# Bucket codes beside the second burst of sums over V, and softmax denominators by chunk

## The chip, the cores and the metric

The kernel runs as one program on one core of a Trainium2 chip. The metric is the device time of one execution in microseconds (us), median of three runs. TensorE is called PE here (PEld for its weight loads), VectorE DVE, ScalarE ACT, GpSimd POOL; SP issues most DMAs. A time in a trace is counted from the start of the profiled span.

## The reference, cut to what matters

Attention in which a query sees only the keys of its own hash bucket, then two gated two-matrix layers on the result. B, H, S, D are 2, 8, 768, 64.

```python
q_bits = (np.einsum('bhsd,dk->bhsk', q, proj) > 0)      # 6 bits each; the same for k
mask = q_bucket[:, :, :, None] == k_bucket[:, :, None, :]
scores = np.where(mask, scale * q @ k.T, -1e9)
attn = np.exp(scores - scores.max(-1))
attn = attn / (attn.sum(-1) + 1e-9)
x = (attn @ v)                                          # to (1536, 512)
h = x @ w_in; x = (h * np.tanh(softplus(h))) @ w_out    # first layer, d_ff 2048
h = x @ w2_in; x = (P(h) / (Q(h) + 1e-6)) @ w2_out      # second layer, P cubic, Q quadratic
```

The result has 1536 rows of 512. Both layers are computed with each operand split into a high and a low part, three products in place of one.

## The kernel before

**Attention.** There are 16 heads, and the work of each is cut into six chunks of 128 keys. `run` goes through slots of time: slot g holds, for every entry of the table `order`, the call whose place falls on g. An entry has the place of head 0, and six slots later comes the next head. So slot 6h + c does chunk c of the scores of head h, and beside it the maxima of a head further on, the sums of the same head some slots late, and the preparation of heads two and three further on. Within a slot the calls are issued in the order of the table, and every engine runs its own instructions in the order in which they were issued. I call the slots of a head 0 to 5; slot 7 of a head is slot 1 of the next.

What a slot issues, by the names that stand in the profile:

- `st` (L373): the tile `sp`, scores with the keys on the partitions, four matmuls of 384 columns (high and low part of the queries, two halves of 384 positions); then ACT takes the exponential into the tile `e`.
- `smax` (L340): the tile `mp`, the same scores with the queries on the partitions, two matmuls; then DVE takes the maximum into `m`.
- `pv` (L391): sums over V of one chunk, out of `e`, two matmuls of 384 columns in float32, each of which writes 64 partitions, so that the two run beside each other in two strips of the array. Three bursts of two chunks each stand in slots 3, 5 and 7 of a head.
- `dsum` (L400): the denominators, the tile `dn`. Four matmuls with a weight of 32 columns of ones stand in four strips of the array. They take two chunks at once, each chunk in two halves of 384 positions; the two halves of partitions are added later by DVE.
- `codes` (L298): the projections of a head's keys and queries, the tile `cp`, in two strips as in `pv`. DVE makes the key rows of it (`code_k`, L320, the tile `kk`), ACT the signs of the query rows (`code_q`, L329, the tile `qB`).
- `vsum` (L268): the sum of V, the tile `vsp`, for two heads together, in slot 3 of every even head; DVE scales it into `vsc`.
- `evac`, `devac`, `gather`, `recip`, `store`, `spread`, `norm`: the results of `pv` and `dn` go out of PSUM, the denominators through two small DMAs (L440) onto 24 partitions, DVE inverts them, and they come back over DRAM.

A float32 matmul stands twice in the trace (two passes), a float32r matmul once. The tiles `sp`, `mp` and `vsp` share a pool of three PSUM buffers: a new tile can be written when the reader of the tile that had its buffer is done, which is ACT for `sp` and DVE for `mp` and `vsp`. The framework decides at build time which buffer a new tile gets; mostly it is the one of three tiles before. `dn` and `cp` share one buffer (L301, L404).

**The layers.** `moe` follows (L632). For each of 3 blocks of 512 rows and 16 slices of d_ff it does 12 matmuls of the first matrix and 12 of the second; the gating runs on ACT and DVE. Beside the first steps DVE rebuilds weights from the 64-bit input (L100 to L106), and `tail` (L626) issues the last slots of attention between them.

The lines that set the places which the change touches:

```python
("lo", lo, -15, 1),
("codes", codes, -16, 1),
("pv", pv, (3, 3, 5, 5, 7, 7), 6),
("dsum", dsum, (5, 5, 5, 5, 7, 7), 6),
("vsum", vsum, 3, 0),
("code_k", code_k, -16, 1),
("code_q", code_q, -14, 1),
```

Of the kernel before, what the change touches and what calls it, by code (L numbers as in the profile page):

```python
# [9 lines left out]
F32 = mybir.dt.float32  # L10
# [3 lines left out]
ACT = mybir.ActivationFunctionType  # L14
ALU = mybir.AluOpType
# [3 lines left out]
B, H, S, D = 2, 8, 768, 64  # L19
# [3 lines left out]
HALF = S // 2  # L23
BLK = 512
NBLK = NT // BLK
NC = S // 128
# [6 lines left out]
    lo="dd", hi="aa", xhi="a", xlo="dd", whi="pppp", wlo="pppp",  # L33
)
C_AT = 16
ROW, TINY = 31, 2.0 ** -60
# [8 lines left out]
def attention_moe_moe(ctx: ExitStack, tc: tile.TileContext, kq, v, proj2, cst, eye, w1, w2, ab, out):  # L45
    nc = tc.nc

    def pool(stack, name, bufs=1, **kw):
        return stack.enter_context(tc.tile_pool(name=name, bufs=bufs, **kw))
# [120 lines left out]
    def attention(actx, tctx):  # L170
        ev_p = pool(tctx, "ev", 2, side="right")
        rx_p = pool(tctx, "rx", 1, side="right")
        cs_p = pool(tctx, "cs", 2, side="right")
# [20 lines left out]
        ones = v_p.tile([128, 32], F32, tag="ones", name="ones")  # L194
# [86 lines left out]
        def qhalf(t, a):  # L281
            return t[:, a * HALF:(a + 1) * HALF]
# [88 lines left out]
        pt = {}  # L371
# [16 lines left out]
        pvt = {}  # L388
# [9 lines left out]


        def dsum(h, c):  # L400
            if not 0 <= h < B * H or c % 2 == 0:
                return
            if c == 1:
                pvt[h, "d"] = pvp.tile([128, 512], F32, tag="dn", name="dn")  # L404
            for n in range(4):
                nc.tensor.matmul(  # L406
                    out=pvt[h, "d"][32 * n:32 * n + 32, 0:HALF], lhsT=ones, rhs=qhalf(pt[h, c - 1 + n // 2], n % 2),
                    start=(c == 1), stop=(c == NC - 1),
                )

        Rt = {}
# [15 lines left out]
        def devac(h):  # L427
            if not 0 <= h < B * H:
                return
            dv = cs_p.tile([128, HALF], F32, tag="dv", name="dv")  # L430
            nc.scalar.activation(out=dv, in_=pvt.pop((h, "d"))[:, 0:HALF], func=ACT.Copy)
            Rt[h] = dv

        def gather(h):
            if not 0 <= h < B * H:
                return
            dv = Rt.pop(h)
            cs = cs_p.tile([24, 2, 32], F32, tag="cs", name="cs")
            for n in range(2):
                nc.sync.dma_start(  # L440
                    out=cs[:, n], in_=dv[64 * n:64 * n + 64:32].rearrange("t (a i) -> t a i", i=32)
                )
            Rt[h] = cs

        def recip(h):
            if not 0 <= h < B * H:
                return
            cs = Rt.pop(h)
            rc = cs_p.tile([24, 32], F32, tag="rc", name="rc")

            z = cs_p.tile([24, 32], F32, tag="z", name="z")
            nc.vector.tensor_tensor(out=rc, in0=cs[:, 0], in1=cs[:, 1], op=ALU.add)
            nc.vector.tensor_scalar(
                out=z, in0=rc, scalar1=0.0, scalar2=float(np.float32(1e-9)) / (S * TINY) - 1.0, op0=ALU.is_equal, op1=ALU.mult
            )
            nc.vector.tensor_scalar(out=rc, in0=rc, scalar1=1e-9, scalar2=None, op0=ALU.add)
            nc.vector.reciprocal(out=rc, in_=rc)
            nc.vector.scalar_tensor_tensor(out=rc, in0=z, scalar=1.0, in1=rc, op0=ALU.add, op1=ALU.mult)
            Rt[h, "r"] = rc
# [52 lines left out]
        for n, p in enumerate(parts):  # L512
            i = W_AT + 6 * n
# [10 lines left out]
        def first(f, n):  # L524
# [18 lines left out]
            ("fin_b", fin_b, -5, 1),  # L543
            ("hi", hi, -18, 1),
            ("move_k", move_k, -17, 1),
            ("lo", lo, -15, 1),
            ("codes", codes, -16, 1),
            ("pv", pv, (3, 3, 5, 5, 7, 7), 6),
            ("dsum", dsum, (5, 5, 5, 5, 7, 7), 6),
            ("vsum", vsum, 3, 0),  # L550
            ("code_k", code_k, -16, 1),
            ("code_q", code_q, -14, 1),
            ("evac", evac, 7, 1),
            ("devac", devac, 7, 1),
            ("gather", gather, 8, 1),
            ("recip", recip, 10, 1),
            ("store", store, 11, 1),
            ("spread", spread, 12, 1),
# [298 lines left out]
    with tc.manual_schedule():  # L857
        nc.scalar.preload_act_table_set("natural_log_exp_and_others")
        tctx = ExitStack()
        with ExitStack() as actx:  # L860
            run, tail = attention(actx, tctx)
            run()
        with ExitStack() as mctx:
            run = moe(mctx, tctx, tail)
            run()
# [55 lines left out]
```

## Time and profile before

| | |
|---|---|
| median of 3 runs | 793.1 us (792.79 to 796.85) |
| profiled execution: time, span | 791.69 us, 789.8 us |
| mean granted TensorE clock | 0.999 |
| busy PE, PEld, DVE, ACT, POOL | 774.2, 572.4, 593.7, 422.5, 71.6 us |

PE has its first matmul of the layers at 259.65 us; what is before that is attention. A busy time counts overlapping instructions once, and matmuls overlap, so the 98% of PE does not say how fast it works. What a group of matmuls costs is read from the start of its first to the start of the next group in the timeline. A row of the timeline is start, time, engine, line, operation, tiles, shapes, count, and in brackets the idle time ahead of it with what ended it; what stands there as a count is of passes.

### The profile page before, as it was taken

The page shows a single profiled execution, that of the slowest core. Times are in us where ns is not written, and L with a number is a line of the kernel's source. Part 1 is how long each engine was busy: PE and PEld are TensorE (multiplying, and loading weights), DVE is VectorE, ACT ScalarE, POOL GpSimd, SP SyncE. Part 2 cuts the span into 40 slices and gives each one's busy share as a digit, 9 for nine tenths or more (in the row PEclk, how much of TensorE's full clock was granted, in tenths as well). Part 3 has the DMA queues.
Part 4 walks back from the last instruction along what each step waited for, and adds up shares of the span by engine and source line. Part 5 has one row for each costly group of instructions (what it writes and reads, how often), then busy time and mean ns, then how long its engine had stood idle before and what let it go on. Part 6 is the DMA issues. An engine that isn't in the chain of part 4 may idle for free.

```text
span 789.8 us, 10934 instructions
## 1 busy us (share of the span) xinstructions
PE 774.2 (98%) x3788; PEld 572.4 (72%) x3788; DVE 593.7 (75%) x1100; ACT 422.5 (53%) x684; POOL 71.6 (9%) x100
## 2 busy tenths in 40 slices
PE   7899999999999999999999999999999999999998
PEld 4556555555555778888888888887888888888886
DVE  5587778778772599846556677659998888888886
ACT  3455565655555443331212334368886867777664
POOL 4223214124121000000000000000000000000000
PEclk9999999999999999999999999999999999999999
DMA  4847666554651444424555587620000100000001
GB/s 124 211 128 202 174 162 175 141 142 121 174 166 31 127 137 148 131 87 145 171 157 149 165 255 256 202 80 1 0 1 1 53 1 1 1 36 18 1 0 54
DMA packets 57031, 85.50 MB, mean 108 GB/s; under 512 B 20496, under 2 KB 28688, under 8 KB 56976
## 3 DMA queue, kind: packets, MB, share of 16 engines
q1 hardware_dynamic: 55952, 84.77, 36.4%
q8 instruction: 30, 0.49, 0.3%
q14 instruction: 25, 0.20, 0.1%
q0 software_dynamic: 1024, 0.03, 0.1%
HBM read 57.71 MB, written 14.73 MB: 92 GB/s over the span
## 4 chain that ended last, share of the span: by engine, by line
PE 88%; DVE 6%; DMA 2%; ACT 1%; issue 1%; SPq 1%; POOL 0%; DVEq 0%; ACTq 0%
PE h L665 29%; PE y L685 16%; PE y L683 15%; PE sp L380 9%; PE pv L287 8%; PE mp L347 5%; PE dn L406 4%; PE cp L287 2%; DVE w L70 1%; DVE m L351 1%; DMA kk<-qB 1%; DVE t L103 1%; DMA vf<-v 1%; DVE r L106 1%; DVE gl L70 1%
## 5 line engine op out<-in xcount | busy, mean ns | idle before, releaser
L665 PE MATMUL h<-xh,w 128*128 128x512 f32 x768 | 205.0, 389 | 0.0
L665 PEld LDWEIGHTS h<-xh,w 128*128 128x128 f32 x768 | 144.1, 188 | 30.6 <-issue 0.6
L351 DVE TENSOR_REDUCE m<-mp 128x1 f32<-128x768 f32 x96 | 91.3, 955 | 50.2 <-PE mp L347 49.0
L385 ACT ACTIVATE e<-sp 128x768 f32<-128x768 f32 x96 | 77.1, 810 | 80.8 <-PE sp L380 79.4
L70 DVE TENSOR_TENSOR gl<-ep,gh 128x512 fp32r<-128x512 f32 x96 | 65.9, 687 | 69.4 <-ACT ep L709 68.6
L708 ACT ACTIVATE gh<-h 128x512 fp32r<-128x512 f32 x48 | 28.7, 598 | 154.7 <-PE h L665 141.5
L665 PE MATMUL h<-xl,w 128*128 128x512 f32 x384 | 102.7, 389 | 0.0
L685 PE MATMUL y<-w,gh 128*128 128x512 f32 x384 | 96.3, 389 | 0.0
L683 PE MATMUL y<-gh,w 128*128 128x512 f32 x384 | 94.8, 389 | 0.0
L665 PEld LDWEIGHTS h<-xl,w 128*128 128x128 f32 x384 | 72.1, 188 | 15.1
L683 PEld LDWEIGHTS y<-gh,w 128*128 128x128 f32 x384 | 72.1, 188 | 15.0
L685 PEld LDWEIGHTS y<-w,gh 128*128 128x128 f32 x384 | 72.1, 188 | 15.0
L287 PE MATMUL pv<-e,vf 128*64 128x384 f32 x384 | 72.5, 499 | 0.0
L380 PE MATMUL sp<-qB,kk 128*128 128x384 f32 x192 | 55.5, 370 | 1.6 <-DMA qB<-stt 1.1
L715 ACT ACTIVATE ep<-h 128x512 f32<-128x512 f32 x48 | 28.5, 595 | 52.3 <-PE h L665 52.3
L347 PE MATMUL mp<-kk,qB 128*128 128x384 f32 x192 | 52.8, 358 | 3.2 <-DVE m L351 2.3
L106 DVE SCALAR_TENSOR_TENSOR r<-r,t 128x256 int32<-128x256 int32 (+1 forms) x114 | 52.2, 457 | 4.7
L380 PEld LDWEIGHTS sp<-qB,kk 128*128 128x128 f32 x192 | 30.8, 188 | 34.1 <-issue 16.0
L103 DVE SCALAR_TENSOR_TENSOR t<-r,t 128x256 int32<-128x256 int32 (+1 forms) x114 | 52.2, 458 | 3.9
L685 PE MATMUL y<-w,gl 128*128 128x512 f32 x192 | 53.3, 392 | 0.5 <-DVE gl L70 0.4
L717 DVE TENSOR_TENSOR n<-n,ep 128x512 f32<-128x512 f32 x48 | 33.1, 690 | 26.9 <-ACT n L716 26.9
L683 PE MATMUL y<-gl,w 128*128 128x512 f32 x192 | 51.6, 390 | 1.6 <-DVE gl L70 1.6
(79 smaller groups left out, 1012.2 us busy)
## 6 DMA issues: line engine op xcount, KB each, us to landing
r<-w SPq DMA_DIRECT2D x100, 256.0 KB
w<-r SPq DMA_DIRECT2D x64, 128.0 KB
w<-w SPq DMA_DIRECT2D x16, 512.0 KB
r<-w SPq DMA_DIRECT2D x14, 512.0 KB
kq<-kq SPq DMA_DIRECT2D x16, 384.0 KB
kk<-qB SPq DMA_DIRECT2D x15, 384.0 KB
kk<-qX SPq DMA_DIRECT2D x16, 192.0 KB
qX<-qB SPq DMA_DIRECT2D x16, 192.0 KB
```

Of the source, the lines that this page charges most:

```text
L70: nc.vector.tensor_tensor(out=o, in0=i, in1=f32(h), op=ALU.subtract)
L103: lambda: nc.vector.scalar_tensor_tensor(out=t, in0=r[:, :, 1], scalar=-0x40000000, in1=t, op0=ALU.bitwise_and, op1=ALU.bitwise_or),
L106: lambda: nc.vector.scalar_tensor_tensor(out=o, in0=r[:, :, 0], scalar=29, in1=t, op0=ALU.logical_shift_right, op1=ALU.bitwise_or),
L287: nc.tensor.matmul(out=o[64 * a:64 * a + 64, 0:HALF], lhsT=w, rhs=qhalf(x, a), start=start, stop=stop)
L347: nc.tensor.matmul(out=p[:, a, 0:HALF], lhsT=qB[h % 4][:, c * 128:(c + 1) * 128], rhs=qhalf(KK[h % 4][:, 0], a), start=True, stop=True,)
L351: nc.vector.tensor_reduce(out=mt[h][:, c:c + 1], in_=halves(p), op=ALU.max, axis=AX.XY)
L380: nc.tensor.matmul(out=p[:, a, 0:HALF], lhsT=kk[:, c * 128:(c + 1) * 128], rhs=qq[:, a * HALF:(a + 1) * HALF], start=(i == 0), stop=(i == 1),)
L385: nc.scalar.activation(out=wide(e), in_=halves(p), func=ACT.Exp, scale=1.0 / D ** 0.5)
L665: nc.tensor.matmul(out=p, lhsT=w[:, c * 128:(c + 1) * 128], rhs=x[:, c, :], start=(n == 0), stop=(n == 11))
L683: nc.tensor.matmul(out=y[m], lhsT=w[:, DM + m * 128:DM + (m + 1) * 128], rhs=g, **s)
L685: nc.tensor.matmul(out=y[m], lhsT=g[:, m * 128:(m + 1) * 128], rhs=w[:, DM:2 * DM], **s)
L717: nc.vector.tensor_tensor(out=v_, in0=v_, in1=u, op=ALU.mult)
```

## The change

`codes` moves from slot 2 to slot 3 of a head, where it is issued directly ahead of the burst of `pv`, and `code_k` and `code_q` move to the same slot. `lo` goes one slot ahead. `dsum` takes one chunk per call, in four quarters of 192 positions, so a head has 24 matmuls of 192 columns in place of 12 of 384. `dv` has 192 columns, `gather` is one DMA in place of two, and the addition of two halves in `recip` is gone.

```diff
-            if not 0 <= h < B * H or c % 2 == 0:
+            if not 0 <= h < B * H:
                 return
-            if c == 1:
+            if c == 0:
                 pvt[h, "d"] = pvp.tile([128, 512], F32, tag="dn", name="dn")
             for n in range(4):
                 nc.tensor.matmul(
-                    out=pvt[h, "d"][32 * n:32 * n + 32, 0:HALF], lhsT=ones, rhs=qhalf(pt[h, c - 1 + n // 2], n % 2),
-                    start=(c == 1), stop=(c == NC - 1),
+                    out=pvt[h, "d"][32 * n:32 * n + 32, 0:S // 4], lhsT=ones,
+                    rhs=pt[h, c][:, n * S // 4:(n + 1) * S // 4], start=(c == 0), stop=(c == NC - 1),
                 )
...
-            cs = cs_p.tile([24, 2, 32], F32, tag="cs", name="cs")
-            for n in range(2):
-                nc.sync.dma_start(
-                    out=cs[:, n], in_=dv[64 * n:64 * n + 64:32].rearrange("t (a i) -> t a i", i=32)
-                )
+            cs = cs_p.tile([24, 32], F32, tag="cs", name="cs")
+            nc.sync.dma_start(out=cs, in_=dv[0:128:32].rearrange("t (a i) -> t a i", i=32))
...
-            nc.vector.tensor_tensor(out=rc, in0=cs[:, 0], in1=cs[:, 1], op=ALU.add)
...
-            ("lo", lo, -15, 1),
-            ("codes", codes, -16, 1),
+            ("lo", lo, -16, 1),
+            ("codes", codes, -15, 1),
             ("pv", pv, (3, 3, 5, 5, 7, 7), 6),
             ("dsum", dsum, (5, 5, 5, 5, 7, 7), 6),
             ("vsum", vsum, 3, 0),
-            ("code_k", code_k, -16, 1),
-            ("code_q", code_q, -14, 1),
+            ("code_k", code_k, -15, 1),
+            ("code_q", code_q, -15, 1),
```

On PE, slots 2 and 3 of a head before. What stands in brackets is what the first matmul of a tile waits for: Activation or DVE is the reader of the tile that had its buffer.

```order
L347 MATMUL mp<-kk_130,qB_122 128x384 [waits Activation_49]
L347 MATMUL mp<-kk_130,qB_122 128x384
L287 MATMUL cp<-kq,pr 64x384 [waits Activation_49]
L287 MATMUL cp<-kq,pr 64x384
L380 MATMUL sp<-qB_120,kk_128 128x384 [waits DVE_49]
L380 MATMUL sp<-qB_120,kk_128 128x384
L380 MATMUL sp<-qX_124,kk_128 128x384 x2
L347 MATMUL mp<-kk_130,qB_122 128x384 [waits Activation_49]
L347 MATMUL mp<-kk_130,qB_122 128x384
L287 MATMUL pv<-e,vf_131 64x384 x4
```

The same place now:

```order
L347 MATMUL mp<-kk_130,qB_122 128x384 [waits Activation_49]
L347 MATMUL mp<-kk_130,qB_122 128x384
L380 MATMUL sp<-qB_120,kk_128 128x384 [waits DVE_49]
L380 MATMUL sp<-qB_120,kk_128 128x384
L380 MATMUL sp<-qX_124,kk_128 128x384 x2
L347 MATMUL mp<-kk_130,qB_122 128x384 [waits Activation_49]
L347 MATMUL mp<-kk_130,qB_122 128x384
L287 MATMUL cp<-kq,pr 64x384 x2
L287 MATMUL pv<-e,vf_131 64x384 x4
```

The two matmuls of `cp` went behind the `mp` of slot 3, so that slots 2 and 3 follow each other as `sp`, `mp`, `sp`, `mp`, and `cp` and `pv` have the same strips.

On PE, slot 5 of the same head before:

```order
L380 MATMUL sp<-qB_120,kk_128 128x384 [waits DVE_49]
L380 MATMUL sp<-qB_120,kk_128 128x384
L380 MATMUL sp<-qX_124,kk_128 128x384 x2
L347 MATMUL mp<-kk_130,qB_122 128x384 [waits Activation_49]
L347 MATMUL mp<-kk_130,qB_122 128x384
L287 MATMUL pv<-e,vf_131 64x384 x4
L406 MATMUL dn<-e,ones 32x384 [waits Activation_49]
```

And now:

```order
L380 MATMUL sp<-qB_120,kk_128 128x384 [waits DVE_49]
L380 MATMUL sp<-qB_120,kk_128 128x384
L380 MATMUL sp<-qX_124,kk_128 128x384 x2
L347 MATMUL mp<-kk_130,qB_122 128x384 [waits DVE_49]
L347 MATMUL mp<-kk_130,qB_122 128x384
L287 MATMUL pv<-e,vf_131 64x384 x4
L406 MATMUL dn<-e,ones 32x192 [waits Activation_49]
```

The `mp` of slot 5 no longer takes the buffer of slot 4's `sp` (three tiles before, read by ACT) but that of slot 4's `mp` (two tiles before, read by DVE). The built program has this in slot 5 of heads 1 to 12. In slot 1 of heads 4, 6, 8, 10 and 12 it is the other way: there `mp` took the buffer of slot 0's `mp` before, and now takes that of slot 0's `sp`.

On DVE, slots 2 to 4 of an even head before; `qX` is `lo`, `kk` is `code_k`:

```order
L351 TENSOR_REDUCE m<-mp 128x1
L324 TENSOR_SCALAR kk_128<-cp,cst 32x384 x2
L351 TENSOR_REDUCE m<-mp 128x1
L70 TENSOR_TENSOR qX_124<-kq,qB_120 128x768
L279 TENSOR_SCALAR vsc<-vsp 128x2
L351 TENSOR_REDUCE m<-mp 128x1
```

And now:

```order
L351 TENSOR_REDUCE m<-mp 128x1
L70 TENSOR_TENSOR qX_124<-kq,qB_120 128x768
L351 TENSOR_REDUCE m<-mp 128x1
L279 TENSOR_SCALAR vsc<-vsp 128x2
L324 TENSOR_SCALAR kk_128<-cp,cst 32x384 x2
L351 TENSOR_REDUCE m<-mp 128x1
```

The two operations of `code_k` and `lo` changed places, and in an even head `code_k` stands behind `vsc`, directly ahead of the maximum of slot 4.

## Rows read from the trace of the kernel before

**Rows 1.** The page, part 4: the chain by engine.

```profile
PE 88%; DVE 6%; DMA 2%; ACT 1%; issue 1%; SPq 1%; POOL 0%; DVEq 0%; ACTq 0%
```

**Rows 2.** Timeline, PE, slots 2 to 5 of an odd head.

```profile
194.24 0.61 PE L380 MATMUL sp<-qB,kk 128*128 128x384 f32 x2
...
195.49 0.87 PE L287 MATMUL cp<-kq,pr 128*64 128x384 f32 x4
196.29 0.62 PE L380 MATMUL sp<-qB,kk 128*128 128x384 f32 x2
...
197.56 1.51 PE L287 MATMUL pv<-e,vf 128*64 128x384 f32 x8
199.00 0.62 PE L380 MATMUL sp<-qB,kk 128*128 128x384 f32 x2
...
200.50 0.51 PE L380 MATMUL sp<-qX,kk 128*128 128x384 f32 x2
200.93 0.62 PE L347 MATMUL mp<-kk,qB 128*128 128x384 f32 x2
201.48 1.51 PE L287 MATMUL pv<-e,vf 128*64 128x384 f32 x8
```

**Rows 3.** Timeline, ACT, two exponentials: slot 4, and slot 0 of an even head.

```profile
200.06 0.81 ACT L385 ACTIVATE e<-sp 128x768 f32<-128x768 f32 x1 [1.88 <-PE sp L380]
...
205.35 0.81 ACT L385 ACTIVATE e<-sp 128x768 f32<-128x768 f32 x1 [0.25 <-PE sp L380]
```

**Rows 4.** Timeline, PE, at three places, in order of time.

```profile
49.10 0.62 PE L347 MATMUL mp<-kk,qB 128*128 128x384 f32 x2
...
186.18 0.61 PE L347 MATMUL mp<-kk,qB 128*128 128x384 f32 x2
...
205.87 0.51 PE L380 MATMUL sp<-qX,kk 128*128 128x384 f32 x2
206.72 0.62 PE L347 MATMUL mp<-kk,qB 128*128 128x384 f32 x2 [0.35 <-DVE m L351]
```

**Rows 5.** Waits in 40 to 240 us: total, times, longest.

```profile
PE mp L347 <- DVE m L351: 1.7, 5, 0.3
```

**Rows 6.** Timeline, ACT, the signs of head 3.

```profile
33.93 1.16 ACT L333 ACTIVATE qB<-cp,cst 32x384 fp32r<-32x384 f32 x2 [3.37 <-DMA kk<-qB]
```

**Rows 7.** Timeline, DVE, at seven places, in order of time.

```profile
43.08 1.82 DVE L351 TENSOR_REDUCE m<-mp 128x1 f32<-128x768 f32 x2 [0.37 <-PE mp L347]
...
184.44 0.16 DVE L279 TENSOR_SCALAR vsc<-vsp 128x2 f32<-128x2 f32 x1
...
196.48 1.34 DVE L324 TENSOR_SCALAR kk<-cp,cst 32x384 fp32r<-32x384 f32 x2
...
198.73 0.95 DVE L70 TENSOR_TENSOR qX<-kq,qB 128x768 fp32r<-128x768 f32 x1
200.35 0.96 DVE L351 TENSOR_REDUCE m<-mp 128x1 f32<-128x768 f32 x1 [0.68 <-PE mp L347]
201.23 0.17 DVE L452 TENSOR_TENSOR rc<-cs 24x32 f32<-24x32 f32 x1
...
205.71 0.96 DVE L351 TENSOR_REDUCE m<-mp 128x1 f32<-128x768 f32 x1 [1.58 <-PE mp L347]
```

**Rows 8.** Timeline, PE: matmuls of 128 columns with a weight of 32 columns.

```profile
14.93 1.50 PE L318 MATMUL wm<-wones,ones 128*32 128x128 f32 x12
```

**Rows 9.** Windows, L406 alone: stretch, length, PE busy and count, PEld the same.

```profile
202.91:202.95 0.04, 0.03 (x4) 0.03 (x5) 1.00 0.95 359
```

**Rows 10.** Timeline, DMA issues of SP, ahead of the first loads of the layers.

```profile
260.68 1.07 SPq L440 DMA_DIRECT2D cs<-dv  x2
261.80 0.88 SPq L774 DMA_DIRECT2D r<-w  x2
```

**Rows 11.** Timeline, DVE, the first rebuilt weights of the layers.

```profile
265.04 0.30 DVE L100 TENSOR_SCALAR t<-r 128x256 int32<-128x256 int32 x1 [0.47 <-DMA r<-w]
```

**Rows 12.** Timeline, PE, a wait in the layers.

```profile
290.79 0.50 PE L683 MATMUL y<-gl,w 128*128 128x512 f32 x1 [1.60 <-DVE gl L70]
```

More of the change, by code (lines that the diff above doesn't have):

```diff
@@ L429, in devac @@
                 return
-            dv = cs_p.tile([128, HALF], F32, tag="dv", name="dv")
-            nc.scalar.activation(out=dv, in_=pvt.pop((h, "d"))[:, 0:HALF], func=ACT.Copy)
+            dv = cs_p.tile([128, S // 4], F32, tag="dv", name="dv")
+            nc.scalar.activation(out=dv, in_=pvt.pop((h, "d"))[:, 0:S // 4], func=ACT.Copy)
             Rt[h] = dv
@@ L451, in recip @@
             z = cs_p.tile([24, 32], F32, tag="z", name="z")
-            nc.vector.tensor_tensor(out=rc, in0=cs[:, 0], in1=cs[:, 1], op=ALU.add)
             nc.vector.tensor_scalar(
-                out=z, in0=rc, scalar1=0.0, scalar2=float(np.float32(1e-9)) / (S * TINY) - 1.0, op0=ALU.is_equal, op1=ALU.mult
+                out=z, in0=cs, scalar1=0.0, scalar2=float(np.float32(1e-9)) / (S * TINY) - 1.0, op0=ALU.is_equal, op1=ALU.mult
             )
-            nc.vector.tensor_scalar(out=rc, in0=rc, scalar1=1e-9, scalar2=None, op0=ALU.add)
+            nc.vector.tensor_scalar(out=rc, in0=cs, scalar1=1e-9, scalar2=None, op0=ALU.add)
             nc.vector.reciprocal(out=rc, in_=rc)
```

## The prediction

> **What bounds the kernel now.** I read the page's chain first: 88% of the time that ends last is PE's, 6% DVE's [rows 1]. So an edit counts by what it does to the times at which PE's matmul groups start, and work on ACT or DVE only where PE waits for it. Next I read PE's timeline over one head [rows 2]. The groups follow each other with almost no idle time, and a group that changes the shape of the strips costs more than its matmuls: `cp` with 4 passes takes 0.80 us up to the next group (195.49 to 196.29), `pv` with 8 passes 1.44 (197.56 to 199.00). The four more passes are two pairs, so a pair costs (1.44 - 0.80)/2 = 0.32, and 0.16 of each group is the way into another shape and out. Last I read where PE does wait. In slots 4 and 5, which follow each other as `sp`, `mp`, `sp`, `mp`, the second `mp` starts 0.43 after the passes ahead of it (200.50 to 200.93), because slot 4's exponential, 200.06 + 0.81, has to end first [rows 2, 3]. In slot 1 of five heads there is a longer wait, for a maximum on DVE [rows 4, 5].
>
> **The codes, on PE.** Slots 2 and 3 now take 199.00 - 194.24 = 4.76 us [rows 2]. After the change they begin like slots 4 and 5: 200.93 - 199.00 = 1.93 up to the second `mp`, the wait for the exponential included, and 201.48 - 200.93 = 0.55 to the next group. That group is `cp` and `pv` in one shape: two pairs more, 0.64 + 1.44. Sum 4.56, so 0.20 is gained per head. The bounds: if `pv` behind `cp` still pays the 0.16, the gain is 0.04; if the exponential were not waited for, some 0.2 more is gained. I take 0.20, since each piece has its row. It holds for 11 heads: -2.2 us. Head 0 gains nothing: its denominators need the buffer of the codes of head 3, whose signs wait 3.37 for a DMA and end at 33.93 + 1.16 [rows 6], and that DMA is issued in the same order as before.
>
> **The maxima, on PE.** The move changes which PSUM buffer a tile gets. In slot 5 of heads 1 to 12, `mp` now waits for the maximum of slot 4 in place of the exponential. In an odd head DVE has time: its work of slots 2 and 3 is in sum what it was, and it stood idle 0.68 ahead of that maximum [rows 7]. It ends at 200.35 + 0.96 = 201.31, and PE follows 0.05 later, as behind the maximum that ends at 205.71 + 0.96 (206.72) [rows 4, 7]. So `mp` starts at 201.36, not 200.93: +0.43. Behind this matmul PE has `pv` and `dn` queued, which nothing overtakes. Five odd heads, 3 to 11: +2.15.
>
> In an even head `code_k` now stands in DVE's queue behind `vsc`, which waits for `vsp`, and ahead of the maximum of slot 4. `vsc` ends at 184.44 + 0.16; with about 0.04 between, `code_k` takes 1.34, and 0.03 later comes the maximum with 0.96: 186.97, and PE at 187.02 where it stood at 186.18 [rows 4, 7]. That is +0.84, for six heads +5.0.
>
> In head 1 two heads' maxima are due in slots 2 and 3, so DVE has a chain of its own from 43.08: 1.82 for two maxima, `lo` 0.95, 1.82 again, `code_k` 1.34, the maximum of slot 4 with 0.96. With 0.3 for the two small operations and overlaps that is 7.1 to 7.2, so PE at 50.2 in place of 49.10 [rows 4, 7]: +1.1 for this head in all, its gain from the codes included.
>
> In slot 1 of five even heads the wait goes the other way. `mp` started 0.85 after the passes ahead (205.87 to 206.72), 0.05 behind the maximum [rows 4, 7]; there are five such waits [rows 5]. Now it needs the exponential of slot 0, 205.35 + 0.81 = 206.16 [rows 3], and starts at 206.21: -0.51 each, -2.5. If DVE stayed the releaser, 0.
>
> **The denominators.** A head had 6 rounds of four strips with 384 columns, and has 12 with 192. A pair of 384 columns costs 0.32, as above. For a round of 192 the nearest row is the one of 12 matmuls with 128 columns and the same 32 columns of weight, 1.50 in all with the tail of the last [rows 8], so at most 0.125 each, and in proportion to 0.32 it would be 0.107. Between 128 and 384 columns in line, a round of 192 costs 0.16 to 0.17, and 12 of them 1.95 to 2.04 where there were 1.93. I take +0.2 for all 16 heads; the bounds are -0.2, and +31 if a shorter round took as long as a longer one (6 x 0.32 x 16). The lower end is near, because the row of 128 columns shows the weight load hidden behind still less streaming.
>
> What speaks against it is the number of instructions: a round now brings four weight loads and four matmuls in 0.16 us. In the trace four matmuls start within 0.04 us [rows 9], which is what waits in the queue, not a lasting rate.
>
> The Trainium skill ("TensorE: Matmul & The Clock Gate", section "Wait — 56ns, not 53.3ns?") says that with hardware decoding off the sequencer spends about 62 ns per matmul, and that this binds where the array's work per matmul is less. By it a round would take 0.25 and all heads some 16 us more, unless the queue covers it. No run here shows a lasting rate under 0.08 us per matmul, so the rule stays a rival.
>
> **DVE and SP.** The addition that goes costs 0.20 from start to start (0.17 and a gap) [rows 7], and one DMA issue of SP is 1.12/2 = 0.56 [rows 10]. Within attention PE waits for neither. Where the layers begin, DVE has a chain of work whose start waited 0.47 for weights loaded behind the two gathers [rows 11], and at its end PE waits 1.60 for DVE [rows 12]. One gather less starts the chain 0.47 earlier (DVE has its other work ahead of it), one addition less shortens it by 0.20: -0.67. If the load comes no sooner, -0.2. The shorter `dv` frees ACT earlier, but the exponential behind it waits for PE: nothing.
>
> **Sum.** -2.2 + 1.1 + 2.15 + 5.0 - 2.5 + 0.2 - 0.67 = +3.1 us on the profiled execution's 791.69, so 794.8. The median of the runs stands 1.4 above the profiled one; on it the sum gives 793.1 + 3.1 = 796.2.
>
> **Rivals.**
>
> 1. *The maxima cost nothing.* If `mp` in slot 5 were not held by DVE, 12 x -0.20 - 2.5 + 0.2 - 0.67 = -5.4 remains: 787.7. For it: PE's groups are read as bound by matmuls, and all the removed pieces lie on PE. Against: the wait is in the built program, and the same wait in slot 1 shows its price. Chance 0.15.
> 2. *Even heads as odd ones.* If DVE reaches `code_k` early enough, say because `vsp` ends sooner than by the old distance, the even heads cost 0.43 like the odd: 3.1 - 6 x 0.41 = +0.6, 793.7. For it: DVE stood idle there. Against: `vsc` waits for PE, and 1.34 us of `code_k` stand behind it. Chance 0.15.
> 3. *The short rounds starve.* If PE cannot be handed 8 instructions in 0.16 us, a round takes 0.25, and 12 x 16 x 0.085 = +16 come on top: 812, or less where the queue covers part of it. It decides from the point at which a burst of `dn` has used up what was queued. Against: 16 passes of `pv` ahead of it are slow and let the queue fill. Chance 0.07.
>
> **How the numbers follow.** The forecast has 0.55, by itself 794 to 798; 0.08 is for what I have not seen, spread over all three outcomes. Within 0.5% (about 4 us, what a measurement of this kernel can tell from no change) lie the second rival, two thirds of the forecast and a share of the unseen: 0.55. Slower by more are the upper third of the forecast, the third rival and a share of the unseen: 0.29. Faster by more is the first rival with the rest: 0.16. The range 787.5 to 799.5 reaches down to the first rival and leaves out the third and most of the unseen.
>
> **What would show it.** In the changed profile: `cp` and `pv` as one run of passes on L287, 12 passes with no break; the second `mp` of slots 4 and 5 with a releaser `m` on DVE, at some 0.87 after the passes ahead in odd heads and 1.2 in even ones; no such wait in slot 1; slots 2 and 3 at 4.56; a burst of `dn` with 32 passes in about 1.43 to the next group; the wait at the start of the layers near 1 us. The forecast is wrong if even heads show no more than 0.87, if `dn` with 32 passes takes over 1.6, or if slots 2 and 3 stay at 4.7.

## The result, and the profile after

| | before | after |
|---|---|---|
| median of 22 runs each | 792.76 us | 797.46 us |
| ratio, 95% interval | | 1.0052 [1.0039, 1.0066] |
| profiled execution: time, span | 791.69, 789.8 us | 799.85, 797.9 us |
| first `sp` to first matmul of the layers | 239.98 us | 244.46 us |
| first matmul of the layers to the end | 530.15 us | 529.44 us |

By the ratio the changed kernel is slower by 0.5%, which is 4.1 us (the two medians lie 4.7 apart), and the forecast was 3.1. The two profiled executions differ by 8.1 us, but 4.3 of these are not the change: the first `sp` starts at 19.67 us in one and at 24.00 in the other, and what is ahead of it is the same in both kernels (experiments with the change start it at 18.9 to 21.1, one without the moved codes at 24.0). What is left is +4.5 in attention and -0.7 in the layers, 3.8 us, which fits the ratio.

In the page's chain of the changed kernel DVE has 12%, where it had 6 [rows 1]:

```profile
PE 82%; DVE 12%; DMA 2%; issue 1%; ACT 1%; SPq 0%; POOL 0%; DVEq 0%; ACTq 0%
```

PE's waits for a maximum from 40 to 240 us (total, times, longest) are twelve with 7.2 us, one in slot 5 of each of heads 1 to 12, where there were five with 1.7, all in slot 1 [rows 5]:

```profile
PE mp L347 <- DVE m L351: 7.2, 12, 0.8
```

This is PE's timeline of slots 2 to 5 of an odd head (11), to be compared with [rows 2]:

```profile
202.58 0.61 PE L380 MATMUL sp<-qB,kk 128*128 128x384 f32 x2
...
204.51 0.61 PE L347 MATMUL mp<-kk,qB 128*128 128x384 f32 x2
205.06 0.87 PE L287 MATMUL cp<-kq,pr 128*64 128x384 f32 x4
205.76 1.46 PE L287 MATMUL pv<-e,vf 128*64 128x384 f32 x8
207.15 0.62 PE L380 MATMUL sp<-qB,kk 128*128 128x384 f32 x2
...
208.64 0.51 PE L380 MATMUL sp<-qX,kk 128*128 128x384 f32 x2
209.65 0.62 PE L347 MATMUL mp<-kk,qB 128*128 128x384 f32 x2 [0.49 <-DVE m L351]
```

Slots 2 and 3 take 207.15 - 202.58 = 4.57 (they took 4.76), `cp` and `pv` together 2.09. In slot 5 `mp` stands 1.01 behind the passes ahead of it, where it stood 0.43.

This is DVE in the same slots (compare [rows 7]):

```profile
204.82 1.65 DVE L70 TENSOR_TENSOR qX<-kq,qB 128x768 fp32r<-128x768 f32 x1
206.39 0.94 DVE L351 TENSOR_REDUCE m<-mp 128x1 f32<-128x768 f32 x1
207.26 1.34 DVE L324 TENSOR_SCALAR kk<-cp,cst 32x384 fp32r<-32x384 f32 x2
208.63 0.96 DVE L351 TENSOR_REDUCE m<-mp 128x1 f32<-128x768 f32 x1
```

`lo` (the `qX` row) takes 1.65 where it took 0.95, and DVE has no idle time between it and the maximum of slot 4, where it had 0.68. Two more engines belong to this place. This is POOL's row that lies beside `lo`:

```profile
204.37 1.28 POOL L67 TENSOR_TENSOR w<-r,w 128x512 fp32r<-128x512 f32 x1
```

In odd head 7 POOL's operation starts only 0.10 ahead of `lo`, which then takes 2.00, and `mp` stands 1.35 behind its passes (146.51), the longest of the twelve waits:

```profile
142.59 1.28 POOL L67 TENSOR_TENSOR w<-r,w 128x512 fp32r<-128x512 f32 x1
142.69 2.00 DVE L70 TENSOR_TENSOR qX<-kq,qB 128x768 fp32r<-128x768 f32 x1
147.86 0.62 PE L347 MATMUL mp<-kk,qB 128*128 128x384 f32 x2 [0.84 <-DVE m L351]
```

On ACT the signs stand in head 11 ahead of the exponentials of slots 4 and 5 (compare [rows 3]):

```profile
208.77 1.16 ACT L333 ACTIVATE qB<-cp,cst 32x384 fp32r<-32x384 f32 x2 [3.26 <-DVE kk L324]
209.96 1.51 ACT L385 ACTIVATE e<-sp 128x768 f32<-128x768 f32 x2
```

The signs wait for `code_k` and hold up ACT's queue: slot 4's exponential starts 2.81 behind the start of its `sp` (207.15 to 209.96), where that was 1.06 (199.00 to 200.06 [rows 2, 3]). No step of the prediction speaks of that.

Next come, on PE, a burst of 32 passes of the denominators and the even head (10) behind it, and then DVE in that head:

```profile
180.74 1.51 PE L406 MATMUL dn<-e,ones 128*32 128x192 f32 x32
182.18 0.62 PE L380 MATMUL sp<-qB,kk 128*128 128x384 f32 x2
...
193.34 0.51 PE L380 MATMUL sp<-qX,kk 128*128 128x384 f32 x2
194.50 0.62 PE L347 MATMUL mp<-kk,qB 128*128 128x384 f32 x2 [0.66 <-DVE m L351]
...
197.93 0.62 PE L380 MATMUL sp<-qB,kk 128*128 128x384 f32 x2
```

```profile
192.04 0.16 DVE L279 TENSOR_SCALAR vsc<-vsp 128x2 f32<-128x2 f32 x1 [0.46 <-PE vsp L274]
192.12 1.34 DVE L324 TENSOR_SCALAR kk<-cp,cst 32x384 fp32r<-32x384 f32 x2
193.49 0.96 DVE L351 TENSOR_REDUCE m<-mp 128x1 f32<-128x768 f32 x1
```

`mp` comes 1.16 behind the passes, as `vsc`, `code_k` and the maximum follow one another. The head takes 197.93 - 182.18 = 15.75. The burst takes 182.18 - 180.74 = 1.44 us up to the next group. The wait in the layers is 1.1, where it was 1.6 [rows 12]:

```profile
PE y L679 <- DVE gl L70: 1.1, 1, 1.1
```

### The profile page after: what moved, and what is told of

The parts are those of the page before. It is cut to its first block, busy times and chain, and to the rows that moved or that the text cites. A ratio compares the mean times of both kernels' runs of the same rounds, so it can differ in the third digit from the quotient of the medians.

```text
span 797.9 us, 11630 instructions
## 1 busy us (share of the span) xinstructions
PE 776.7 (97%) x4172; PEld 587.2 (74%) x4172; DVE 596.4 (75%) x1084; ACT 418.5 (52%) x684; POOL 71.5 (9%) x100
## 4 chain that ended last, share of the span: by engine, by line
PE 82%; DVE 12%; DMA 2%; issue 1%; ACT 1%; SPq 0%; POOL 0%; DVEq 0%; ACTq 0%
PE h L661 29%; PE y L681 15%; PE y L679 14%; PE pv L287 7%; PE sp L380 6%; PE dn L406 4%; PE mp L347 4%; DVE m L351 3%; DVE kk L324 2%; DVE qX L70 1%; PE cp L287 1%; DMA kk<-qB 1%; DVE w L70 1%; DMA r<-w 1%; DVE t L103 1%
## 5 line engine op out<-in xcount | busy, mean ns | idle before, releaser
L347 PE MATMUL mp<-kk,qB 128*128 128x384 f32 x192 | 56.1, 376 | 9.3 <-DVE m L351 8.4
L347 PEld LDWEIGHTS mp<-kk,qB 128*128 128x128 f32 x192 | 32.7, 194 | 23.0 <-DVE m L351 14.5
```

Source lines behind the costliest of these rows:

```text
L347: nc.tensor.matmul(out=p[:, a, 0:HALF], lhsT=qB[h % 4][:, c * 128:(c + 1) * 128], rhs=qhalf(KK[h % 4][:, 0], a), start=True, stop=True,)
```

## The experiments

All times of heads are from the start of the first `sp` of a head to that of the next, in PE's timeline, for an even head (10) and an odd one (11). The attention column runs from the first `sp` to the first matmul of the layers. Numbers 1, 2 and 10 still have the wait in slot 1 in heads 4, 6 and 8, which take some 0.5 us more than head 10 (16.2, 15.7 and 15.5).

| kernel | even | odd | attention | ratio to before, 95% |
|---|---|---|---|---|
| before | 15.72 | 14.76 | 239.98 | 1 |
| after | 15.75 | 15.14 | 244.46 | 1.0052 [1.0039, 1.0066] |
| 1 codes only | 15.76 | 15.13 | 245.32 | 1.0065 [1.0043, 1.0088] |
| 2 quarters only | 15.22 | 14.78 | 238.49 | 1.0001 [0.9982, 1.0019] |
| 3 vsum behind code_k | 15.46 | 15.13 | 243.00 | 1.0029 [1.0010, 1.0048] |
| 4 lo in slot 3 | 15.76 | 15.00 | 243.64 | 1.0034 [1.0017, 1.0051] |
| 5 after, buffers in turn | 16.92 | 16.32 | 267.51 | 1.0336 [1.0307, 1.0364] |
| 6 before, buffers in turn | 15.18 | 14.76 | 238.98 | 0.9962 [0.9942, 0.9982] |
| 7 quarters only, buffers in turn | 15.23 | 14.79 | 240.03 | 0.9964 [0.9942, 0.9985] |
| 8 as 5, early matmuls | | | 268.62 | 1.0336 [1.0311, 1.0361] |
| 9 as 5, signs in slot 4 | 15.04 | 14.56 | 236.90 | 0.9938 [0.9913, 0.9962] |
| 10 after, signs in slot 4 | 15.02 | 14.56 | 238.16 | 0.9960 [0.9941, 0.9979] |
| 11 as 9, early matmuls | 15.03 | 14.59 | 237.38 | 0.9950 [0.9932, 0.9968] |

**1. The codes alone.**

```diff
-            ("lo", lo, -15, 1),
-            ("codes", codes, -16, 1),
+            ("lo", lo, -16, 1),
+            ("codes", codes, -15, 1),
-            ("code_k", code_k, -16, 1),
-            ("code_q", code_q, -14, 1),
+            ("code_k", code_k, -15, 1),
+            ("code_q", code_q, -15, 1),
```

> The kernel before with only the four places in the table changed (codes, code_k, code_q and lo); the denominators stay two chunks at a time. In the built program slot 5 of heads 1 to 12 has the new buffer for mp, and slot 1 of heads 4, 6 and 8 keeps its wait for a maximum (10 and 12 lose it). Theory (the loss is the wait of mp in slot 5 for slot 4's maximum): time up by 5 to 6.5 us, ratio 1.006 to 1.008; slots 2 and 3 of an odd head at 4.57 us; that mp 1.0 us behind the passes ahead of it in odd heads and 1.16 in even ones; the wait where the layers begin stays at 1.6 to 1.8. Rival (the loss is the 24 short matmuls of the denominators): the move alone gains 0.2 us per head, ratio 0.994 to 0.998.

These are PE's waits for a maximum from 40 to 240 us:

```profile
PE mp L347 <- DVE m L351: 7.7, 15, 0.7
```

There are fifteen, twelve in slot 5 and three in slot 1, and the whole loss is here: attention is 5.3 us longer than before. The move carries the loss.

**2. The denominators alone:** the changed kernel with those four entries of the table as they were.

> The changed kernel with the four places in the table put back to those of before: only the denominators by chunk, one gather and no addition are left of the change. In the built program slot 1 of heads 10 and 12 loses its wait for a maximum, 4, 6 and 8 keep it, and slot 5 is as before. Theory (the loss is the wait in slot 5): two waits of 0.5 us less, the layers start 0.7 us sooner, the bursts of dn cost 0.03 us more per head: -1.2 us, ratio 0.997 to 1.000; a burst of 32 passes takes 1.44 us. Rival (the short matmuls cost): the loss is here, ratio 1.004 to 1.02.

Attention is 1.5 us shorter (two waits of 0.5 gone, and a head 0 that is 0.7 shorter), and the layers 0.65 shorter. The median shows none of it; this kernel's runs lie 5.5 us apart (789.99 to 795.45), and the lower half of the ratio's interval overlaps with what was expected. A cost of the short matmuls of 0.4% or more, as the rival has it, is excluded.

**3. `vsum` behind `code_k`.**

```diff
-            ("vsum", vsum, 3, 0),
             ("code_k", code_k, -15, 1),
+            ("vsum", vsum, 3, 0),
```

> The changed kernel with the entry vsum moved behind code_k in the table, so that on DVE the two operations of code_k no longer stand behind vsc, which waits for PE. Theory (in even heads code_k, held by vsc, delays slot 4's maximum): that maximum ends 0.5 us sooner in an even head, the mp of slot 5 starts some 0.65 us behind the passes ahead of it instead of 1.16, six heads give 2.5 to 3.3 us back; ratio to before 1.001 to 1.003. Rival (the maximum is late because DVE is full, in even heads as in odd ones): mp stays at 1.0 to 1.16 and the ratio at 1.005.

This is DVE and then PE in head 10:

```profile
185.50 1.34 DVE L324 TENSOR_SCALAR kk<-cp,cst 32x384 fp32r<-32x384 f32 x2
186.88 0.16 DVE L279 TENSOR_SCALAR vsc<-vsp 128x2 f32<-128x2 f32 x1
187.20 0.96 DVE L351 TENSOR_REDUCE m<-mp 128x1 f32<-128x768 f32 x1 [0.16 <-PE mp L347]
```

```profile
187.09 0.62 PE L380 MATMUL sp<-qB,kk 128*128 128x384 f32 x2
187.55 0.51 PE L380 MATMUL sp<-qX,kk 128*128 128x384 f32 x2
188.21 0.62 PE L347 MATMUL mp<-kk,qB 128*128 128x384 f32 x2 [0.16 <-DVE m L351]
```

`mp` comes 0.66 behind the passes, as expected, but the head gains 0.30 and not 0.5: slot 5's `sp` has the buffer of `vsp` and starts at 187.09, behind the late `vsc` (186.88 + 0.16). Attention is 1.5 us shorter than in the changed kernel, where 2.5 to 3.3 were expected. The order on DVE in even heads is shown as a cause, and part of the gain turns into another wait.

**4. `lo` back in slot 3.**

```diff
-            ("lo", lo, -16, 1),
+            ("lo", lo, -15, 1),
```

> The changed kernel with lo put back into slot 3. In the changed kernel lo took 1.65 us on DVE in slot 2, where it stands beside two operations of POOL, and 0.95 before. Theory (two operations with two inputs each, one on DVE and one on POOL, hold each other up): lo takes 0.95 again in slot 3, the maximum of slot 4 ends 0.3 us sooner in odd heads, mp in slot 5 starts 0.65 to 0.75 behind the passes ahead instead of 1.0; even heads stay at 1.16, because vsc waits for PE; in all -1.5 us, ratio to before 1.003 to 1.005. Rival (lo is slower for another reason, its data or its place behind the maximum): 1.65 in the new slot too, and no gain.

```profile
201.04 0.95 DVE L70 TENSOR_TENSOR qX<-kq,qB 128x768 fp32r<-128x768 f32 x1
201.91 1.35 DVE L324 TENSOR_SCALAR kk<-cp,cst 32x384 fp32r<-32x384 f32 x2
203.50 0.96 DVE L351 TENSOR_REDUCE m<-mp 128x1 f32<-128x768 f32 x1 [0.24 <-PE mp L347]
```

```profile
203.65 0.51 PE L380 MATMUL sp<-qX,kk 128*128 128x384 f32 x2
204.51 0.62 PE L347 MATMUL mp<-kk,qB 128*128 128x384 f32 x2 [0.35 <-DVE m L351]
```

`lo` takes 0.95 again, and DVE is idle ahead of slot 4's maximum. `mp` stands 0.86 behind, not at the 0.65 to 0.75 expected: with DVE free the maximum still has to wait for its own `mp`, and that is the forecast's 0.87. So of the 0.58 by which `mp` comes later in an odd head, 0.15 is `lo` and 0.43 the buffer. Attention is 0.8 us shorter than in the changed kernel, where 1.5 was expected.

**5 and 6. Buffers strictly in turn,** in the changed kernel (5) and in the one before (6). The same is done for `sp`, `vsp` and the tile of the first warming matmuls.

```diff
+        turn = [0]
+        def rot(name):
+            turn[0] += 1
+            return ps.tile([128, 2, 512], F32, tag=f"s{turn[0] % 3}", name=name, bufs=1)
...
-            p = ps.tile([128, 2, 512], F32, tag="s", name="mp")
+            p = rot("mp")
```

> The changed kernel with the three PSUM buffers of sp, mp and vsp taken strictly in turn (a new tile gets the buffer of three tiles before), so that mp in slot 5 has the buffer of slot 4's sp again. Theory (the buffer decides, and the move of the codes by itself gains): mp in slot 5 starts 0.43 us behind the passes ahead of it, odd heads take 14.55 us instead of 15.11, even ones 15.0 instead of 15.75, attention 7.8 us less than in the changed kernel and 3.3 less than before; ratio to before 0.994 to 0.997. Rival (DVE is too full for the new order, whatever the buffers): the wait comes back at the next sp or mp that takes a buffer of a maximum, ratio 1.000 to 1.005.

> The kernel before with the three PSUM buffers taken strictly in turn. Theory (the five waits in slot 1 are there only by the choice of buffers): all five go, even heads take 15.2 us as heads 10 and 12 do where only the denominators are changed, -2.5 us, ratio 0.995 to 0.999. Rival (those maxima are late anyway, and a later tile waits): no change, ratio 0.999 to 1.001.

Number 6 does what was expected: the waits in slot 1 are gone and with them 0.54 of each of those heads. Number 5 contradicts the theory as I had put it: 27 us slower. This is PE and then ACT in head 11 (ACT's first row are the signs):

```profile
223.39 0.51 PE L386 MATMUL sp<-qX,kk 128*128 128x384 f32 x2
225.53 0.62 PE L353 MATMUL mp<-kk,qB 128*128 128x384 f32 x2 [1.63 <-ACT e L391]
```

```profile
223.48 1.16 ACT L339 ACTIVATE qB<-cp,cst 32x384 fp32r<-32x384 f32 x2 [3.25 <-DVE kk L330]
224.67 1.51 ACT L391 ACTIVATE e<-sp 128x768 f32<-128x768 f32 x2
```

With the exponential as releaser `mp` stands 2.14 behind its passes, because the exponential itself is late, behind the signs. So in this order the maximum, which the framework had chosen, was the cheaper of two late releasers; what makes the exponential late is another part of the change. Over heads 1 to 12 `mp` stands 14.3 us further behind its passes, in sum, than in the changed kernel. Head 0 takes 5.4 more. Heads 6 and 12 take some 1.6 more than the other even heads, with a lower clock behind their waits:

```profile
138.40:140.50 2.10, 0.30 (x2) 0.00 (x0) 1.97 (x5) 1.98 (x4) 1.04 (x2) 1.00 1.08 314
140.50:144.20 3.70, 3.67 (x14) 1.24 (x18) 1.89 (x3) 0.68 (x1) 1.16 (x2) 0.54 0.85 265
```

These are two windows of number 5, in head 6: stretch, length, busy times and counts of PE, PEld, DVE, ACT and POOL, then PEclk, DMA share and GB/s. PE is busy 0.30 of 2.10 us, and in the 3.7 us behind that the granted clock is 0.54, about the 1.2 GHz level.

**7. Quarters only, buffers in turn:** number 5 with the four entries of the table as before.

> The kernel with buffers in turn and denominators by chunk, but with codes, code_k, code_q and lo at their places of before. Beside the one with buffers in turn and all of the change it shows what the place of the codes is worth by itself. Theory (0.2 us per head for the way in and out of another shape): odd heads 14.77 us and even ones 15.22 here, 14.55 and 15.0 there; against before -3.2 us here, ratio 0.995 to 0.999. Rival (the shape costs nothing by itself): the same head times in both.

The heads take what was expected. `code_q` stands in slot 4 here as in number 9, so the two show what the place of `cp` is worth (`code_k` and `lo` move with it): 14.79 - 14.56 = 0.23 and 15.23 - 15.04 = 0.19 per head.

**9 and 10. The signs back in slot 4,** with buffers in turn and with the framework's.

```diff
-            ("code_q", code_q, -15, 1),
+            ("code_q", code_q, -14, 1),
```

> The changed kernel with buffers in turn (which took 27 us more than before) and code_q back in slot 4, that is, behind the exponential of slot 4 on ACT. Theory (in the changed kernel the signs stand ahead of slot 4's exponential on ACT and wait for code_k on DVE, so that this exponential starts 2.7 us late, whichever buffer mp takes): the exponential of slot 4 starts as soon as its sp is done, mp in slot 5 starts 0.43 us behind the passes ahead of it, odd heads take 14.55 us and even ones 15.0; against before -5 to -6 us, ratio 0.991 to 0.995. Rival (buffers in turn don't go with the codes at their new place, whatever ACT does): the loss stays, ratio over 1.02. Second rival (DVE is too full): ratio 1.000 to 1.005.

> The changed kernel with code_q alone put back into slot 4; the buffers are as the framework chooses them, and in the built program mp in slot 5 now gets the buffer of slot 4's sp again, and slot 1 of heads 4, 6 and 8 its wait for a maximum. Theory (the place of the signs is what costs: it delays the exponential, and the choice of slot 4's maximum as releaser follows from it): odd heads 14.57 us, even ones 15.0 (heads 4, 6 and 8 15.5), attention 2 us below before and the layers 0.5 us sooner; ratio to before 0.995 to 0.999. Rival (code_k on DVE costs, the signs don't): odd heads stay at 15.1 and even ones at 15.75, ratio 1.004 to 1.006.

This is number 9 in head 11: ACT, PE, and DVE's maximum of slot 4.

```profile
197.37 0.81 ACT L391 ACTIVATE e<-sp 128x768 f32<-128x768 f32 x1 [2.70 <-PE sp L386]
198.21 1.16 ACT L339 ACTIVATE qB<-cp,cst 32x384 fp32r<-32x384 f32 x2
```

```profile
196.31 0.62 PE L386 MATMUL sp<-qB,kk 128*128 128x384 f32 x2
...
197.81 0.51 PE L386 MATMUL sp<-qX,kk 128*128 128x384 f32 x2
198.24 0.61 PE L353 MATMUL mp<-kk,qB 128*128 128x384 f32 x2
```

```profile
197.79 0.96 DVE L357 TENSOR_REDUCE m<-mp 128x1 f32<-128x768 f32 x1
```

The exponential waits for its `sp` alone, `mp` stands 0.43 behind, and the heads take what was foreseen within 0.04 us. `lo` still takes 1.64 there and DVE still runs through from `code_k` to the maximum. From the start of slot 4's `sp` (196.31) the maximum ends after 2.44 us, as in the changed kernel (207.15 to 209.59), while the exponential starts after 1.06 and no longer after 2.81. So the signs make the exponential late and not the maximum; the late maximum costs nothing as long as `mp` does not have its buffer. In number 10 one line of the table turns a loss of 0.5% into a gain of 0.4%; the framework then picks slot 4's `sp` for `mp` by itself, and three waits for a maximum are left, all in slot 1:

```profile
PE mp L347 <- DVE m L351: 1.1, 3, 0.4
```

Number 9 has the lowest ratio of all kernels that were run, 0.9938, but its interval overlaps with those of 6, 7, 10 and 11.

**8 and 11. Three early matmuls,** added to 5 and to 9.

```diff
-            ("khi", 0, 0), ("lo", 0), ("code_q", 0), ...
+            ("warm", 3, True), ("khi", 0, 0), ("lo", 0), ("code_q", 0), ...
```

> As the kernel with all of the change and buffers in turn, with three matmuls of 128 columns more where TensorE waits from 7.0 to 8.2 us for the first signs; they write a buffer of the first warming ones and wait for nothing. In some profiles the matmuls from 8.2 to 18 us take twice as long as in others, and the first sp starts at 24.0 in place of 19.7. Theory (the clock rises late because TensorE stood idle there): the first sp always starts near 19.7, all runs lie within 1.5 us, median 2 us below the same kernel without these matmuls. Rival (the moment at which the clock rises does not depend on this wait): the same spread of 5 us.

> The kernel with buffers in turn and the signs in slot 4 (ratio 0.994) with the three early matmuls in TensorE's first wait. Theory (without that wait the fast pace always comes by 11 us): the first sp starts at 20.5 at the latest, all runs lie within 2.5 us of each other where that kernel's lay within 3.9, median 787 to 788, ratio 0.991 to 0.994. Rival (the early matmuls only cost their own time): the same spread, median 788.5 to 790.

Number 8 was expected 2 us below number 5, with all runs within 1.5 us; its median is 0.4 below, and its runs lie 2.5 apart (819.47 to 821.97), where those of number 5 lie 3.2 apart. Number 11 was expected at 787 to 788 and has 788.79, above number 9; its runs lie 2.4 apart (787.85 to 790.22), where those of number 9 lie 3.9 apart. No gain in time is shown, and whether the spread is smaller is left open.

## Why the prediction was right, and where it was not

- **The codes on PE: right.** 4.56 was forecast for slots 2 and 3, 4.57 measured, `cp` and `pv` in one shape at 2.09 for 2.08. Numbers 7 and 9 show the 0.20 by itself.
- **The denominators: right.** 1.44 for 1.43. The third rival is out: 32 passes and their weight loads within 1.44 us are 0.045 us each. The Trainium skill ("TensorE: Matmul & The Clock Gate", section "Wait — 56ns, not 53.3ns?") has about 62 ns per matmul with hardware decoding off, by which 32 passes would take an estimated 1.98; these passes in four strips are faster than that. No run here shows whether hardware decoding was on.
- **Even heads: right, a little too dear.** 1.16 for 1.2, by the order of DVE that the prediction gives; number 3 confirms it. The second rival is out.
- **Odd heads: mechanism right, term too small.** 1.01 for 0.87. The step that failed is "its work of slots 2 and 3 is in sum what it was": `lo` grew from 0.95 to 1.65 beside POOL's operation. Number 4, without that, has 0.86. In head 7, where `lo` takes 2.00, it is 1.35.
- **Slot 1: right.** The five waits are gone; number 6 gives 15.72 - 15.18 = 0.54 for 0.51.
- **The layers: right.** The wait is 0.5 shorter, the stretch 0.71, for 0.67. What the gather and what the addition gave of it was not separated.
- **Head 1** +0.99 for +1.1. **Head 0** (first `sp` to first `sp`) 17.37 for 16.90, where no change was forecast; its denominators still wait for signs that wait for a DMA. Why that takes 0.47 longer stays open: the starts of the two executions differ, and the kernels without the moved codes range from 16.2 to 18.9.
- **The sum: close in part by luck.** By the lengths of heads (codes, maxima and slot 1 together) the five odd heads 3 to 11 cost 2.2 us for 1.15, and the six even heads 2 to 12 cost 0.8 for 1.34. Head 0 cost 0.47 where nothing was forecast. Errors of both signs leave 3.8 for 3.1.
- **Two slips in the working.** Twelve rounds of 0.16 are 1.92 and not 1.95, and the burst of `pv` ahead of `dn` has 8 passes [rows 2] and not 16, as the third rival has it. Neither changes the forecast.
- **The first rival: right to be unlikely, wrong in its price.** It supposed that with the exponential as releaser `mp` would start 0.43 behind. The prediction asked what changes on ACT only for the shorter `dv`, "the exponential behind it waits for PE: nothing", and did not see that `code_q`, moved one slot ahead, stands in front of slot 4's exponential and waits for `code_k`. Number 5 shows the real price, +27 us in place of -5.4, and number 10 that this edit alone decides the sign. The forecast came out because the buffers of the built program were read and not guessed: the maximum was the releaser, and its time was in the trace.

In the trace `code_q` waits for `code_k` (the signs start 0.17 behind its end, 207.26 + 1.34 to 208.77), though both only read `cp`. The Trainium skill ("PSUM — Partial Sum Buffer", section "PSUM bank collisions raise a hardware error") says that two engines may be in one bank at the same time as long as they are in different quadrants of 32 partitions; the key rows and query rows of `cp` are in different ones. Taking that wait away was not tried.

## What to carry to other kernels

When a call is moved, look at every queue that it enters, and at what stands behind it there: a small operation that waits, put one slot ahead of an exponential, costs what the exponential releases. If a buffer is given to the second-best releaser, ask what made the best one late before forcing the rotation. And a gain on the bounding engine (0.2 us per head here) shows only when the releasers around it still come in time: with the signs in their old slot the same change gains 0.4%. With buffers in turn as well it is 0.6%, but 0.4 of that comes with the buffers alone (number 6).

## What the runs showed of the hardware

`lo`, an operation of DVE with two inputs in SBUF, hardly moves while POOL runs one with two inputs. In the changed kernel the eleven `lo` from 65 us on overlap with one of POOL; the row of head 11 above starts 0.45 behind POOL's and takes 1.65. POOL ends at 205.65; 0.95 from there is 206.60, and `lo` ends at 206.47. In head 7 POOL ends at 143.87, which makes 144.82, and `lo` ends at 144.69. The Trainium skill ("SBUF — State Buffer", section "SBUF: two separate sides") says that such a pair holds a shared port in turn, the first for its whole instruction; by it `lo` would end at 206.60 and 144.82, and the trace agrees to 0.13 both times. In the kernel before, `code_k`, with one input and that in PSUM, stood beside POOL's same operation, whose row follows; it took 1.34 at 196.48 [rows 7], as it does now at 207.26, alone.

```profile
196.03 1.29 POOL L67 TENSOR_TENSOR w<-r,w 128x512 fp32r<-128x512 f32 x1
```

At the start TensorE takes longer per matmul, in some executions up to some 18 us. These are rows of PE in the changed kernel's profile, with the same tile at both paces:

```profile
17.00 1.01 PE L347 MATMUL mp<-kk,qB 128*128 128x384 f32 x2
17.93 0.84 PE L318 MATMUL wm<-wones,ones 128*32 128x128 f32 x4
18.71 0.62 PE L347 MATMUL mp<-kk,qB 128*128 128x384 f32 x2
```

In the profile of before, `mp` takes 0.62 from 8.63 on. The windows give PEclk as 1.00 in both, so this column does not show it. Between these two profiles it goes with a first `sp` that is 4.3 us later; whether it makes the spread of the other runs is not shown, since they have no trace. What ended the slow pace at one time or the other was not found.
